# Two operand buffers and seven weight buffers moved to one place modulo 256 bytes in SBUF

## The chip, the cores and the metric

The kernel runs on one NeuronCore of a Trainium2 chip. The metric is device time in microseconds for one launch. Names of engines are those of the profile: PE is the matrix engine, PEld its weight loads (they run beside its matmuls), ACT and DVE the two elementwise engines, POOL the general one, SP the one whose queue issues every DMA of this kernel. SBUF is the on-chip memory of 128 partitions; a buffer begins at the same byte address in every partition. That address modulo 256 is called the buffer's **place** in this document. PSUM is the memory that the matmuls write.

## The reference

Two layers in sequence. The first is attention with a sigmoid in place of the softmax, for 8 batches, 12 heads, 448 positions and head dimension 64. The second is a channel mix with a shift by one position in time.

```python
scores = scale * np.matmul(q, k.transpose(0, 1, 3, 2)) - np.log(S)
attn = 1.0 / (1.0 + np.exp(-scores))
x = np.matmul(attn, v)                      # then heads side by side: (8, 448, 768)
xk = mu_k * x + (1.0 - mu_k) * x_prev       # x_prev is x one position earlier
xr = mu_r * x + (1.0 - mu_r) * x_prev
k = np.maximum(xk @ w_k, 0.0)               # 768 -> 1024
v = k * k @ w_v                             # 1024 -> 768
r = 1.0 / (1.0 + np.exp(-(xr @ w_r)))       # 768 -> 768
return r * v
```

All is float32; the three weight matrices arrive as float64.

## The kernel before, in words

**Attention** (the first 268.6 us of the span). The heads are taken in 48 pairs. Keys and queries are split into a coarse float32r part and a remainder, and a score tile is the sum of three float32r matmuls (coarse by coarse, remainder by coarse, coarse by remainder; `scores`, L338). The two heads of a pair sit in the two halves of the array's rows. The split keys and queries lie in the weight buffers' spare columns (`kk` in slots 0 and 3, `qh` in 1 and 4, `ql` in 2 and 6), because the weight buffers are not full yet. ACT applies the sigmoid (L361), PE weighs the values with it in plain float32 (`weigh`, L368), and ACT and DVE blend each position with the one before (L391, L392). The blended results go to DRAM. Meanwhile the float64 weights come in as raw bits (`wraw`), DVE turns them into float32 (`wbit`), and their combinations are stored to DRAM or put into the slots.

**The three products** (stage 0: `xr @ w_r`, stage 1: `xk @ w_k`, stage 2: `k*k @ w_v`). The 3584 columns are cut into 7 blocks of 512. Each block pair is multiplied with a scheme that needs seven half-size products instead of eight (`ORDER`: products 0, 1, 4, 5, 6, 2, 3); the first, odd block has four plain ones (`SINGLE`: 0, 4, 1, 3). That is 25 products in each stage. Product `p` has its own weight buffer: `slots[POS[p]]`, so in the order of `ORDER` the products use slot 0, 1, 2, 3, 4, 5, 6, and in that of `SINGLE` slot 0, 2, 1, 6. A slot holds a coarse half `hi` and a remainder `lo`, each 1152 or 1536 float32r numbers long in a partition.

The moving operand (512 columns) is split in the same way (`operand`, L453 on ACT and L454 on DVE) into one of two buffers: `rra`, allocated at the kernel's start, or `rrb`, allocated in the attention's space after that is freed. `take` deals them out: in stages 0 and 1 coarse part and remainder of one operand lie in the same buffer, two operands in `rra`, the next two in `rrb`. In stage 2 every third operand has its coarse part in `rra` and its remainder in `rrb`.

`multiply` (L592) issues one matmul with its weight load for each of the three combinations of parts and each tile of 128 rows:

```python
for e, (a, b) in enumerate(((whi[:, c], hi[:, t]), (whi[:, c], lo[:, t]), (wlo[:, c], hi[:, t]))):
    nc.tensor.matmul(bank, a, b, ...)       # a: 128x128 weights, b: 128x512 moving
```

A product of stage 0 has 27 such matmuls, one of stages 1 and 2 has 36; the three stages have 25 x (27 + 36 + 36) = 2475. Products 0, 1, 4 and 2 write the PSUM banks called `xb`, products 5, 6 and 3 those called `yb` (in a block pair: xb, xb, xb, yb, yb, xb, yb). The order on every engine is fixed beforehand by a planner (`Plan`), which lists each operation with a cost and a priority and emits them sorted by the start that it works out. It knows no addresses.

**Where the buffers lie.** The left side of SBUF holds a small constant pool that ends at byte 16672 and then the pool `wp`. Everything in it is a multiple of 256 bytes long, apart from the two tiles called `gap` and the 8 numbers (32 bytes) by which a slot is longer than its content. Every tile of weights and every part of an operand begins a multiple of 256 bytes behind the start of its buffer, so one number gives the place of all that PE reads from it.

Of the kernel before, what the change touches and what calls it, by code (L numbers as in the profile page):

```python
# [8 lines left out]
F32 = mybir.dt.float32  # L9
F32R = mybir.dt.float32r  # L10
# [88 lines left out]
def attention_then_channel_mix(  # L99
# [16 lines left out]
    P = 128  # L116
# [16 lines left out]
    WO = NJH * DF // 2  # L133
# [27 lines left out]
    def ring(pool, name, bufs, shape, dtype):  # L161
        return [pool.tile(shape, dtype, name=f"{name}{i}") for i in range(bufs)]

    wp = ctx.enter_context(tc.tile_pool(name="wp", bufs=1, side="left"))
    att = ExitStack()
    wp.tile([P, 56], F32, name="gap0")
    slots = [wp.tile([P, 2 * WO + 8], F32R, name=f"slot{g}") for g in range(7)]
    wp.tile([P, 8], F32, name="gap1")
    RU = 2 * NJH
    rra = wp.tile([P, 2 * RU, TB], F32R, name="rra")  # L170
    ysa = wp.tile([P, RU, TB], F32, name="ysa")
# [376 lines left out]
    kp = ctx.enter_context(tc.tile_pool(name="kp", bufs=1, side="right", reuse_waits="tile"))  # L548
# [3 lines left out]
    p1s = ring(kp, "p1s", 4, [P, TB], F32)  # L552
    u2 = ring(kp, "u2", 4, [P, TB], F32)
    cc = ring(kp, "cc", 5, [P, TB], F32)
    kp.tile([P, 40], F32, name="gap2")
    pb = ctx.enter_context(tc.tile_pool(name="pb", bufs=1, space=PSUM, reuse_waits="tile"))
    yb = ring(pb, "yb", 4, [P, TB], F32)
    xb = ring(pb, "xb", 4, [P, TB], F32)
# [150 lines left out]
```

## Time and profile before

| | |
|---|---|
| median of 3 runs | 851.38 us (850.54 to 852.36) |
| profiled execution | 849.64 us, of it the span 847.7 us |
| granted PE clock | 1.0 throughout |
| attention, 0 to 268.6 us | PE busy 259.28, DVE 218.51, ACT 202.84, DMA share 0.82 |
| products, 268.6 to 843.3 us | PE busy 574.66 of 574.70, DVE 415.83, ACT 265.77, DMA share 0.56 |
| end, 843.3 to 847.7 us | DVE 1.38, last DMA |

A PE row of the timeline view gives the start of its first matmul, how long it lasted until the modelled end of its last one, the bank written, the moving buffer and the weight buffer (numbers left out) and the count. Because matmuls overlap, the time that a matmul costs is not its own duration but the distance from the start of one row to the start of the next, divided by the count. This is called the **pace** below.

### The profile page before, as it was taken

The numbers are of one execution on the slowest core, as the hardware profiler recorded it, in microseconds if no ns is written. First come the engines' busy times: TensorE is split into PE (matmuls) and PEld (weight loads), VectorE is DVE, ScalarE is ACT, GpSimd is POOL, SyncE is SP. The second block draws the span as 40 slices with busy tenths as digits, with TensorE's granted clock in tenths as the row PEclk, the third lists the DMA queues.
The fourth block names the chain that finished last, engine by engine and source line by source line (L and its number), as shares of the span: only waits on it lengthen the run. The fifth ranks groups of instructions, "written<-read, shape, count | busy, mean of one in ns | idle before, by whom it ended". The sixth has DMA issues, their size and how long they took to land.

```text
span 847.7 us, 12701 instructions
## 1 busy us (share of the span) xinstructions
PE 833.9 (98%) x4299; PEld 591.2 (70%) x4299; DVE 635.7 (75%) x1156; ACT 468.6 (55%) x753; POOL 10.6 (1%) x100
## 2 busy tenths in 40 slices
PE   7999999999989999999999999999999999999997
PEld 4444444444445888888888888888888888888886
DVE  5788989887877889799895375284666748949854
ACT  5788978777775435446447456366574323332320
POOL 0000000000000000000000000000000000000000
PEclk9999999999999999999999999999999999999999
DMA  6778877798987783848784526524755465457304
GB/s 216 248 250 291 292 248 246 252 323 293 311 283 253 278 286 140 256 154 270 268 269 151 173 101 211 161 100 137 272 175 189 133 224 174 136 187 224 124 25 149
DMA packets 97489, 179.64 MB, mean 212 GB/s; under 512 B 12560, under 2 KB 53008, under 8 KB 95632
## 3 DMA queue, kind: packets, MB, share of 16 engines
q1 hardware_dynamic: 97424, 178.83, 63.6%
q8 instruction: 34, 0.56, 0.3%
q14 instruction: 31, 0.25, 0.1%
HBM read 109.06 MB, written 69.73 MB: 211 GB/s over the span
## 4 chain that ended last, share of the span: by engine, by line
PE 94%; DMA 2%; issue 2%; ACT 1%; DVE 1%; DVEq 0%; ACTq 0%
PE xb L592 38%; PE yb L592 30%; PE av L368 12%; PE sc L338 10%; PE av L376 2%; DMA xk_d<-xo 2%; PE sc L349 2%; ACT xo L391 1%; DMA raw<-in_qk 0%; DVE xo L392 0%; ACT pf L361 0%; ACT pt L361 0%; DVE slot L317 0%; DVE cc L647 0%; DVE cc L617 0%
## 5 line engine op out<-in xcount | busy, mean ns | idle before, releaser
L592 PE MATMUL xb<-rra,slot 128*128 128x512 f32 x717 | 177.5, 394 | 0.0
L592 PE MATMUL xb<-rrb,slot 128*128 128x512 f32 x669 | 165.5, 394 | 0.0
L592 PEld LDWEIGHTS xb<-rra,slot 128*128 128x128 f32 x717 | 134.5, 188 | 32.3 <-issue 0.7
L592 PE MATMUL yb<-rra,slot 128*128 128x512 f32 x618 | 154.4, 395 | 0.0
L592 PEld LDWEIGHTS xb<-rrb,slot 128*128 128x128 f32 x669 | 125.6, 188 | 29.3
L361 ACT ACTIVATE pf<-sc 128x896 f32<-128x896 f32 x144 | 123.2, 936 | 22.4 <-PE sc L338 22.4
L592 PEld LDWEIGHTS yb<-rra,slot 128*128 128x128 f32 x618 | 116.3, 188 | 27.3
L368 PE MATMUL av<-pf,vn 128*64 128x448 f32 x576 | 118.6, 547 | 4.5 <-DVE xo L392 4.4
L592 PE MATMUL yb<-rrb,slot 128*128 128x512 f32 x471 | 119.3, 395 | 0.0
L338 PEld LDWEIGHTS sc<-slot,slot 64*128 64x128 f32 x864 | 76.9, 187 | 49.6 <-issue 17.6
L338 PE MATMUL sc<-slot,slot 64*128 64x448 f32 x864 | 106.6, 383 | 4.8 <-DVE slot L317 4.8
L592 PEld LDWEIGHTS yb<-rrb,slot 128*128 128x128 f32 x471 | 88.5, 188 | 21.2
L368 PEld LDWEIGHTS av<-pf,vn 128*64 128x64 f32 x576 | 37.2, 136 | 64.6 <-issue 47.7
L453 ACT CAST rra<-ysa 128x512 fp32r<-128x512 f32 x88 | 52.5, 622 | 51.8 <-PE xb L592 15.0
L454 DVE TENSOR_TENSOR rra<-ysa,rra 128x512 fp32r<-128x512 f32 x76 | 49.9, 686 | 13.0 <-ACT rra L453 12.7
L453 ACT CAST rrb<-ysa 128x512 fp32r<-128x512 f32 x60 | 35.4, 616 | 35.9 <-DVE u L633 10.6
L391 ACT ACTIVATE xo<-av,omr 128x447 f32<-128x447 f32 x48 | 30.7, 639 | 41.5 <-PE av L376 23.4
L318 DVE TENSOR_TENSOR slot<-raw,slot 128x384 fp32r<-128x384 f32 x96 | 52.5, 584 | 0.0
L392 DVE SCALAR_TENSOR_TENSOR xo<-av,mur,xo 128x448 f32<-128x448 f32 x48 | 32.7, 681 | 19.1 <-ACT xo L391 10.7
L633 DVE TENSOR_TENSOR u<-yb,p1s 128x512 f32<-128x512 f32 x30 | 20.7, 691 | 34.9 <-PE yb L592 34.9
L454 DVE TENSOR_TENSOR rrb<-ysa,rrb 128x512 fp32r<-128x512 f32 x60 | 39.0, 684 | 10.4 <-ACT rrb L453 10.1
L578 DVE TENSOR_TENSOR slot<-cc,slot 128x512 fp32r<-128x512 f32 x42 | 28.0, 685 | 19.3 <-ACT slot L577 19.3
(68 smaller groups left out, 789.6 us busy)
## 6 DMA issues: line engine op xcount, KB each, us to landing
raw<-in_qk SPq DMA_DIRECT2D x48, 448.0 KB, 6.4
k_d<-cc SPq DMA_DIRECT2D x56, 256.0 KB, 2.2
vn<-in_v SPq DMA_DIRECT2D x48, 224.0 KB, 2.7
xr_d<-xo SPq DMA_DIRECT2D x48, 224.0 KB, 6.7
xk_d<-xo SPq DMA_DIRECT2D x48, 224.0 KB, 6.5
r_d<-cc SPq DMA_DIRECT2D x42, 256.0 KB, 2.2
out<-cc SPq DMA_DIRECT2D x42, 256.0 KB, 3.1
wraw<-in_moe_w_k SPq DMA_DIRECT2D x12, 512.0 KB, 7.2
```

Of the source, the lines that this page charges most:

```text
L318: op(DVE, dve(w), at, lambda src_=src_, hi=hi, lo=lo: nc.vector.tensor_sub(lo, src_, hi), [R, (key + "h", i)], [(key + "l", i)])
L338: nc.tensor.matmul(sc[u][:, h, :S], kk[i][half[h], int(e == 1), kc], qq[i][half[h], :], start=e == 0, stop=e == 2)
L349: nc.tensor.matmul(sc[u][half[h ^ (m % 2)], m % 2, :S], t[half[h], QKW:], t[half[h], KW:QKW], start=True, stop=True)
L361: op(ACT, act(2 * S), at, lambda: nc.scalar.activation(f, sc[u][:, :, :S], AF.Sigmoid, bias=NEG_LOG_S, scale=SCALE), R, [K])
L368: nc.tensor.matmul(av[n % 2][half[h], :S], vn[n % 5][:, h * NC + c, :], pf[i][:, h, :], start=c == 0, stop=False)
L391: op(ACT, act(S, False, True), at, lambda y=y, om=om: nc.scalar.mul(y[:, 1:], x[:, :S - 1], om[:, j:j + 1]), [("av", n % 2), ("om", key)], ...
L392: op(DVE, dve(S, ptr=True), at - 5, lambda y=y, mu=mu: nc.vector.scalar_tensor_tensor(y, x[:, :S], mu[:, j:j + 1], y, ALU.mult, ALU.add), ...
L453: op(ACT, act(TB, True), at, lambda t=t: nc.scalar.copy(hi[:, t], y[:, t]), [Y[t]], [H[t]])
L454: op(DVE, dve(TB), at, lambda t=t: nc.vector.tensor_sub(lo[:, t], y[:, t], hi[:, t]), [Y[t], H[t]], [L[t]])
L578: op(DVE, dve(TB), at, lambda h_=h_, l_=l_, w=w: nc.vector.tensor_sub(l_, w, h_), [W, K + (h, "hi")], [K + (h, "lo")])
L592: nc.tensor.matmul(bank, a, b, start=first and t == 0 and e == 0, stop=t == n - 1 and e == 2, skip_group_check=True)
L633: op(DVE, dve(TB), at, lambda: add(u2[i], y, p1s[i]), [Y, P1], [U2])
```

## The change

The slots lose their 8 extra numbers, the two gap tiles of the left pool go, and the gap at the end of the right pool `kp` grows from 40 to 48 numbers, which moves that pool's other tiles down by 32 bytes.

```diff
     wp = ctx.enter_context(tc.tile_pool(name="wp", bufs=1, side="left"))
     att = ExitStack()
-    wp.tile([P, 56], F32, name="gap0")
-    slots = [wp.tile([P, 2 * WO + 8], F32R, name=f"slot{g}") for g in range(7)]
-    wp.tile([P, 8], F32, name="gap1")
+    slots = [wp.tile([P, 2 * WO], F32R, name=f"slot{g}") for g in range(7)]
...
     cc = ring(kp, "cc", 5, [P, TB], F32)
-    kp.tile([P, 40], F32, name="gap2")
+    kp.tile([P, 48], F32, name="gap")
     pb = ctx.enter_context(tc.tile_pool(name="pb", bufs=1, space=PSUM, reuse_waits="tile"))
```

The places (byte address modulo 256) in the two built programs:

| buffer | before | after |
|---|---|---|
| slots 0, 1, 2, 3, 4, 5, 6 | 0, 32, 64, 96, 128, 160, 192 | all 32 |
| `rra` (moving operands) | 0 | 32 |
| `rrb` (moving operands) | 64 | 32 |
| `ysa`, `wraw`, `wbit`, `wexpo` | 0 | 32 |
| `ysb`, `p1s`, `u2`, `cc` | 64 | 32 |
| attention's `raw`, `vn`, `pf`, `pt`, `xo` | 224 | 224 |

In all engines' lists the instructions, their order, their shapes and their waits are the same in both programs; they differ in addresses alone.

## The prediction

> **What bounds the kernel now.** I read the busy time by stage first, then the order of PE's matmuls inside the products, then the chain of waits. By stage (columns: span, then busy time and count of PE, PEld, DVE, ACT and POOL, granted clock, DMA share, GB/s):
>
> ```profile
> 0.00:268.60 268.60, 259.28 (x1825) 126.29 (x1825) 218.51 (x459) 202.84 (x289) 10.48 (x99) 1.00 0.82 270
> 268.60:843.30 574.70, 574.66 (x2479) 464.87 (x2475) 415.83 (x697) 265.77 (x464) 0.10 (x1) 1.00 0.56 186
> ```
>
> The second row holds the three products. PE is busy for 574.66 of 574.70 us at the full clock, and all 2475 weight loads fall in it; 574.70 / 2475 = 232.2 ns is what one matmul costs on average. No other engine is near: DVE works 72% of the time. So each nanosecond of pace in these 2475 matmuls is 2.5 us of the kernel, and the question is what the pace hangs on. The timeline of PE shows it, because the name of a row gives the moving buffer, and the sequence of banks gives the product and so the slot:
>
> ```profile
> 500.47 8.58 PE L592 MATMUL xb<-rra,slot 128*128 128x512 f32 x36
> 508.89 8.41 PE L592 MATMUL yb<-rra,slot 128*128 128x512 f32 x36
> 517.14 16.82 PE L592 MATMUL xb<-rrb,slot 128*128 128x512 f32 x72
> ...
> 567.44 8.56 PE L592 MATMUL yb<-rra,slot 128*128 128x512 f32 x36
> 575.84 8.35 PE L592 MATMUL xb<-rra,slot 128*128 128x512 f32 x36
> 584.03 16.76 PE L592 MATMUL xb<-rrb,slot 128*128 128x512 f32 x72
> 600.63 16.96 PE L592 MATMUL yb<-rra,slot 128*128 128x512 f32 x72
> 617.43 8.58 PE L592 MATMUL xb<-rrb,slot 128*128 128x512 f32 x36
> 625.84 8.53 PE L592 MATMUL yb<-rrb,slot 128*128 128x512 f32 x36
> 634.21 8.37 PE L592 MATMUL xb<-rra,slot 128*128 128x512 f32 x36
> 642.42 8.56 PE L592 MATMUL yb<-rra,slot 128*128 128x512 f32 x36
> 650.82 8.55 PE L592 MATMUL xb<-rrb,slot 128*128 128x512 f32 x36
> 659.21 0.39 PE L592 MATMUL yb<-rra,slot 128*128 128x512 f32 x1
> ```
>
> From 575.84 on this is the last block pair of stage 1 (slots 0 to 6) and from 634.21 the first block of stage 2 (slots 0, 2, 1, 6). The rows are of one shape, with nothing idle between them. Start to start, over the count, and beside it the place of the weights less the place of the moving operand (modulo 256):
>
> - 575.84, slot 0 on rra, difference 0: 8.19 / 36 = 227.5 ns. 634.21, the same pair: 8.21 / 36 = 228.1 ns.
> - 642.42, slot 2 on rra, difference 64: 8.40 / 36 = 233.3 ns.
> - 617.43, slot 5 on rrb, difference 96: 8.41 / 36 = 233.6 ns.
> - 625.84, slot 6 on rrb, difference 128: 8.37 / 36 = 232.5 ns.
> - 500.47, slot 5 on rra, difference 160: 8.42 / 36 = 233.9 ns.
> - 508.89, slot 6 on rra, difference 192: 8.25 / 36 = 229.2 ns; 567.44, the same pair: 8.40 / 36 = 233.3 ns.
> - 650.82, slot 1 on rrb, difference 224: 8.39 / 36 = 233.1 ns.
> - 584.03, slot 1 (224) and slot 2 (difference 0, at place 64) on rrb together: 16.60 / 72 = 230.6 ns. With 233.1 for the first, slot 2 is left with 228.1 ns.
>
> The pace is thus a matter of addresses. Where weights and moving operand share a place, be it 0 or 64, it is about 227.8 ns; elsewhere it is 232 to 234, but for one pair that was seen at both 229.2 and 233.3. The before kernel has the shared place in few of its products, since its slots lie at seven different places and its operands at two.
>
> **The change, part by part.**
>
> *Products.* The change gives all weights and all operands place 32, so every one of the 2475 matmuls, the split operands of stage 2 included, has difference 0. If the difference is what counts, each costs 227.8 ns (the mean of 227.5 and 228.1): 2475 x 0.2278 = 563.8 us instead of 574.7, a gain of 10.9. PE never waits in this stretch, so all of it reaches the end as long as the others keep up. The hardest part for DVE is the start:
>
> ```profile
> 260.00:450.00 190.00, 190.00 (x844) 150.41 (x837) 165.96 (x302) 96.14 (x170) 0.44 (x4) 1.00 0.72 243
> ```
>
> DVE has 166 us of work in 190; with PE 2% quicker the same work has 186 us, 89%. That covers it. Were the cover gone and DVE the bound there, the most that could be lost is that stretch's share of the gain, 190 x 1.9% = 3.6 us.
>
> *Attention.* Its score matmuls read slots too. Today their differences (keys in slots 0 and 3, queries in 1, 2, 4 and 6) are 224, 192 and 160, and they become 0. No score matmul at difference 0 is in the trace, so I bound the gain. Two heads' matmuls run side by side, so the 864 of L338 are 432 pairs:
>
> ```profile
> L338 PE MATMUL sc<-slot,slot 64*128 64x448 f32 x864 | 106.6, 383 | 4.8 <-DVE slot L317 4.8
> ...
> 185.62 2.48 PE L368 MATMUL av<-pf,vn 128*64 128x448 f32 x12
> 188.02 2.10 PE L338 MATMUL sc<-slot,slot 64*128 64x448 f32 x18
> 190.05 0.60 PE L368 MATMUL av<-pf,vn 128*64 128x448 f32 x2
> ```
>
> A run of 18 (9 pairs) takes 190.05 - 188.02 = 2.03 us, 225 ns for a pair of only 448 columns, so part of it is not address conflicts but the waits between the planner's operations. If a pair gained the 233.3 - 227.8 = 5.5 ns of the products, 432 of them would gain 2.4 us; if those waits or the attention's stops set the time, nothing. The chain has such stops, in which PE is not the last to arrive:
>
> ```profile
> 99.97 6.78 DMA xk_d<-xo
> 144.54 7.29 DMA xk_d<-xo
> 234.48 3.05 issue x2
> ```
>
> I take 1.0 us, a little under the middle. The other matmuls of the attention (values weighed, score tails) read buffers that stay at place 224.
>
> *Loads, casts, copies.* DMAs and elementwise work now touch place 32 where they touched 0 or 64. The trace has aligned and unaligned neighbours for these:
>
> ```profile
> raw<-in_qk SPq DMA_DIRECT2D x48, 448.0 KB, 6.4
> wraw<-in_moe_w_k SPq DMA_DIRECT2D x12, 512.0 KB, 7.2
> ...
> ysa<-r_d SPq DMA_DIRECT2D x22, 256.0 KB, 3.2
> ysb<-r_d SPq DMA_DIRECT2D x20, 256.0 KB, 3.0
> ...
> L453 ACT CAST rra<-ysa x88: 601/621/711, 79.3 to 795.1; 128x512 fp32r<-128x512 f32 x88
> L453 ACT CAST rrb<-ysa x60: 602/619/647, 270.8 to 784.8; 128x512 fp32r<-128x512 f32 x60
> ```
>
> A load into place 224 moves 448 / 6.4 = 70 KB per us, one into place 0 moves 512 / 7.2 = 71; 256 KB land in place 64 no later than in place 0; a cast into place 0 takes 621 ns, into 64 619. I cost these at nothing; PE's 2475 matmuls hide them, and if the cover were gone, 1.5% (70 against 71) of a 7.2 us load would be 0.1 us.
>
> *Sum.* 10.9 + 1.0 = 11.9 us off the profiled execution's 849.64: 837.7. The median of the runs shown stands 1.7 higher, so 851.38 - 11.9 = **839.5 us**.
>
> **What speaks against it.** After the change both operands lie at place 32, an odd multiple of 32, and no row shows that: the shared places seen are 0 and 64. Odd differences are also slower than their neighbours suggest. Between the even ones (64: 233.3, 128: 232.5, 192: 229.2, 0: 227.8) one would expect 232.9 at 96, 230.9 at 160 and 228.5 at 224; the rows say 233.6, 233.9 and 233.1, or 0.7, 3.0 and 4.6 more, 2.8 on average. In each of these rows exactly one of the two operands is at an odd multiple of 32. It may be the mismatch that costs, which the change removes, or the odd place itself, which it doubles.
>
> **The rivals.**
>
> *The odd place costs on its own, for each operand (slower).* Place: every matmul of L592. Price: two operands at 2.8 ns on top of the shared place, 227.8 + 5.6 = 233.4 ns against 232.2 now, so 2475 x 1.2 ns = 3.0 us more: 854.4 us. It decides from a pace above 232.2. For it: no row with an odd place is under 233. Against it: the rows at differences 64 and 128 have no odd place and are as slow, so oddness isn't needed to explain 233.
>
> *Half of that.* One such price for both operands together: 230.6 ns, 1.6 ns under now, 4.0 us gained, 847.4 us (attention at nothing).
>
> *Places don't matter in themselves (no change): 851.4 us.* The pace would then follow something that goes with the product, such as its place in the block pair or what ACT and DVE do beside it. Against it: 575.84 and 634.21 differ in stage, neighbours and companions and agree to 0.6 ns, and slot 2 is slow on rra (233.3) and quick on rrb (228.1). For it: 508.89 and 567.44, one pair of places at two paces, so the pace has more than one input.
>
> [...]
>
> *A second steady state at the shared place (not quite the gain).* As with 508.89 and 567.44, some products could settle at 233.3. If one in four did, 0.25 x 2475 x 5.5 ns = 3.4 us would be missing: 842.9. All three products at difference 0 in the rows above are quick, so this belongs to the forecast's own spread.
>
> **How the numbers follow.** The forecast, place by difference alone, gets 0.68: its own range is 836.5 (2.4 us in attention and a slightly better pace) to 843. The half price gets 0.12, no change 0.08, the odd place as a loss 0.12. What a measurement of this kernel can tell from no change is about 0.2%, 1.7 us. Faster: 0.68 + 0.12 = 0.80; same 0.08; slower 0.12. The range holds the first two cases and leaves out the others' 0.2: 836 to 849.
>
> **What would show it.** In the changed kernel's timeline every full row of 36 at L592 should stand 8.2 us before the next, whatever its buffers, and the stretch from the first product's matmul to the last should be 564 us with PE still without idle time. Rows of 8.4 throughout mean the odd place costs; a mix of 8.2 and 8.4 means two steady states. Runs of 18 score matmuls should take 1.98 to 2.03 us. If the pace falls but the span doesn't, idle time of PE before L592 would name the engine that is late next, DVE in the first stage before any other. The forecast is wrong if the stretch isn't shorter by at least 7 us.

## The result and the profile after

The changed kernel takes **838.94 us** (median of 4 runs, 838.69 to 839.72) where the kernel before takes 851.87 (4 runs, 850.54 to 853.09): a ratio of 0.985 with a 95% interval of 0.9833 to 0.9867, so 12.9 us or 1.5% faster. The forecast was 839.5.

The profiled execution of the changed kernel took 839.72 us, 837.8 of it the span. By stage (span, then busy time and count of PE, PEld, DVE, ACT and POOL, granted clock, DMA share, GB/s):

```profile
0.00:272.00 272.00, 261.17 (x1824) 127.04 (x1824) 219.83 (x461) 202.76 (x289) 11.04 (x100) 0.99 0.81 267
272.00:833.35 561.35, 561.35 (x2479) 464.60 (x2475) 413.54 (x693) 265.23 (x464) 0.00 (x0) 1.00 0.57 190
```

The products shrank from 574.70 to 561.35 us, 13.35 us less, 226.8 instead of 232.2 ns for each of the 2475 matmuls. PE is busy for all of it, so no engine became late, and the work of DVE and ACT is the same (413.54 and 265.23 us against 415.83 and 265.77). The attention took 3.4 us longer in this execution (272.0 against 268.6); what that is worth is told under the experiments.

The timeline of PE over the last block pair of stage 1 and the first block of stage 2, as it was read before (`multiply` is at L590 now, since two lines fell away; in a stage's first block product 4 writes `yb`, so that its banks come as xb, yb, xb, yb):

```profile
563.90 8.32 PE L590 MATMUL yb<-rra,slot 128*128 128x512 f32 x36
572.07 8.32 PE L590 MATMUL xb<-rra,slot 128*128 128x512 f32 x36
580.23 16.48 PE L590 MATMUL xb<-rrb,slot 128*128 128x512 f32 x72
596.54 16.48 PE L590 MATMUL yb<-rra,slot 128*128 128x512 f32 x72
612.87 8.32 PE L590 MATMUL xb<-rrb,slot 128*128 128x512 f32 x36
621.02 8.32 PE L590 MATMUL yb<-rrb,slot 128*128 128x512 f32 x36
629.18 8.32 PE L590 MATMUL xb<-rra,slot 128*128 128x512 f32 x36
637.35 8.32 PE L590 MATMUL yb<-rra,slot 128*128 128x512 f32 x36
645.50 8.32 PE L590 MATMUL xb<-rrb,slot 128*128 128x512 f32 x36
```

Every row of 36 stands 8.15 to 8.17 us before the next and every row of 72 16.31 to 16.33: 226.4 to 226.9 ns for all slots and both operand buffers. The spread that such rows had before (227.5 to 233.9) is gone.

### The profile page after: what moved, and what is told of

The parts are those of the page before. It is cut to its first block, busy times and chain, and to the rows that moved or that the text cites. A ratio compares the mean times of both kernels' runs of the same rounds, so it can differ in the third digit from the quotient of the medians.

```text
span 837.8 us, 12701 instructions
## 1 busy us (share of the span) xinstructions
PE 822.5 (98%) x4299; PEld 591.6 (71%) x4299; DVE 634.8 (76%) x1156; ACT 468.0 (56%) x753; POOL 11.0 (1%) x100
## 4 chain that ended last, share of the span: by engine, by line
PE 90%; DMA 5%; ACT 2%; issue 1%; DVE 1%; DVEq 0%; SPq 0%; ACTq 0%; POOL 0%; POOLq 0%
PE xb L590 38%; PE yb L590 29%; PE av L366 11%; PE sc L336 9%; DMA xk_d<-xo 4%; PE av L374 2%; PE sc L347 1%; ACT xo L389 1%; ACT pt L359 1%; ACT pf L359 1%; DVE xo L390 1%; DMA raw<-in_qk 0%; DVE slot L315 0%; ACT rra L451 0%; DVE cc L645 0%
## 5 line engine op out<-in xcount | busy, mean ns | idle before, releaser
L590 PE MATMUL xb<-rra,slot 128*128 128x512 f32 x717 | 173.9, 389 | 0.0
L590 PE MATMUL xb<-rrb,slot 128*128 128x512 f32 x669 | 162.2, 389 | 0.0
L590 PEld LDWEIGHTS xb<-rra,slot 128*128 128x128 f32 x717 | 134.5, 188 | 28.6 <-issue 0.7
L590 PE MATMUL yb<-rra,slot 128*128 128x512 f32 x618 | 150.8, 389 | 0.0
L590 PEld LDWEIGHTS xb<-rrb,slot 128*128 128x128 f32 x669 | 125.6, 188 | 26.0
L590 PEld LDWEIGHTS yb<-rra,slot 128*128 128x128 f32 x618 | 116.0, 188 | 24.1
L590 PE MATMUL yb<-rrb,slot 128*128 128x512 f32 x471 | 116.3, 389 | 0.0
L590 PEld LDWEIGHTS yb<-rrb,slot 128*128 128x128 f32 x471 | 88.4, 188 | 18.3
L452 DVE TENSOR_TENSOR rra<-ysa,rra 128x512 fp32r<-128x512 f32 x76 | 49.4, 685 | 11.0 <-ACT rra L451 10.9
```

Source lines behind the costliest of these rows:

```text
L452: op(DVE, dve(TB), at, lambda t=t: nc.vector.tensor_sub(lo[:, t], y[:, t], hi[:, t]), [Y[t], H[t]], [L[t]])
L590: nc.tensor.matmul(bank, a, b, start=first and t == 0 and e == 0, stop=t == n - 1 and e == 2, skip_group_check=True)
```

## The experiments

All paces are read as before, start to start over the count. The diffs are shortened (`...` or a remark marks what is left out). They stand against the changed kernel, and from "Which stream has to walk?" on against the kernel before. Slot and product follow from the sequence of banks.

**One half: the weights at one place.** Slots all at 32, `rra` at 0 and `rrb` at 64 as before.

```diff
     slots = [wp.tile([P, 2 * WO], F32R, name=f"slot{g}") for g in range(7)]
     ...
+    wp.tile([P, 56], F32, name="gap0")          # rra to place 0
     rra = wp.tile([P, 2 * RU, TB], F32R, name="rra")
     ...
-    kp.tile([P, 48], F32, name="gap")
+    kp.tile([P, 40], F32, name="gap")           # rrb to place 64
```

> Slots all at place 32, rra at 0 and rrb at 64 as before: half of the change. Theory (the difference of the places decides): every product has difference 32 or 224, none has 0, so the pace is 233.2 ns throughout, 2475 x (233.2 - 232.2) = 2.5 us slower than before, about 854 us. Rival 1 (it is enough that all weights share a place, because loads follow each other): 226.7 ns as in the changed kernel, 839 us. Rival 2 (both halves add up): half the gain, about 845 us.

Measured: 854.86 us against 850.79, ratio 1.0037 (1.002 to 1.0054). The stretch of the products:

```profile
268.50:846.20 577.70, 577.68 (x2479) 464.38 (x2475) 414.64 (x694) 266.31 (x464) 0.00 (x0) 1.00 0.56 185
```

577.70 / 2475 = 233.4 ns, 3.0 us longer than before. It is not enough that the weights share a place; without difference 0 anywhere, this half alone is a loss.

**The other half: the operands at one place.** `rra` and `rrb` at 32, slots staggered by 32 bytes from 0 to 192.

```diff
-    slots = [wp.tile([P, 2 * WO], F32R, name=f"slot{g}") for g in range(7)]
+    wp.tile([P, 56], F32, name="gap0")
+    slots[0] = wp.tile([P, 2 * WO], F32R, name="slot0")
+    wp.tile([P, 8], F32, name="gap1")           # and so on, 8 before each next slot
+    slots[1] = wp.tile([P, 2 * WO], F32R, name="slot1")
     ...
+    wp.tile([P, 24], F32, name="gap7")          # rra stays at place 32
```

> rra and rrb both at place 32, slots at 0, 32, 64, 96, 128, 160, 192: the other half. Theory (difference): only slot 1 has difference 0 and runs at 226.7 ns; the others have 224, 32, 64, 96, 128 and 160 and run at 232 to 234; weighted by their 4, 4, 4, 3, 3, 3 and 4 products of 25 that is 232.4 ns, as before, 851 to 853 us. Rival (operands that share a place are what helps): all rows at 226.7 ns, 839 us.

Measured: 853.11 us against 850.79, ratio 1.003 (1.0017 to 1.0044). In its timeline the first block of stage 2, with slots 0, 2 and 1 in that order:

```profile
638.40 8.56 PE L605 MATMUL xb<-rra,slot 128*128 128x512 f32 x36
646.80 8.56 PE L605 MATMUL yb<-rra,slot 128*128 128x512 f32 x36
655.20 8.34 PE L605 MATMUL xb<-rrb,slot 128*128 128x512 f32 x36
663.37 0.39 PE L605 MATMUL yb<-rra,slot 128*128 128x512 f32 x1
```

Slot 0 (difference 224) and slot 2 (32) take 8.40 us, 233.3 ns; slot 1 (difference 0) takes 8.17, 226.9 ns. One quick slot of seven is about what the kernel before had, hence no gain. The stretch of the products:

```profile
272.50:847.60 575.10, 575.09 (x2479) 464.85 (x2475) 415.08 (x693) 266.06 (x464) 0.00 (x0) 1.00 0.56 186
```

575.10 us is only 0.4 more than before, so most of the 2.3 us between the medians lies outside the products. In them the two halves do not add up: 3.0 us lost and 0.4 us lost alone, 13.35 us won together. What counts is weights against operand.

**All at place 0 instead of 32.** This tells the difference from the place itself; `rrb` moreover stands 256 bytes off modulo 512.

```diff
+    wp.tile([P, 56], F32, name="gap0")
     slots = [wp.tile([P, 2 * WO], F32R, name=f"slot{g}") for g in range(7)]
     ...
-    kp.tile([P, 48], F32, name="gap")
+    kp.tile([P, 56], F32, name="gap")
```

> Slots, rra and rrb all at place 0; rrb lies 256 modulo 512 from the slots, rra 0 modulo 512. Theory (difference modulo 256 alone): 226.7 ns in every row, whichever buffer, 839 us as with place 32. Rival 1 (place 32 itself is better than 0): rows between 226.7 and 230 ns, up to 847 us. Rival 2 (the period is 512 bytes): rra rows at 226.7, rrb rows at 232 to 234 ns, about 845 us.

Measured: 838.21 us against 850.79, ratio 0.9849 (0.9827 to 0.9871).

```profile
270.80:832.10 561.30, 561.30 (x2479) 464.48 (x2475) 415.63 (x695) 265.45 (x464) 0.10 (x1) 1.00 0.57 190
```

561.30 us against the changed kernel's 561.35, 226.8 ns for each matmul in both: place 0 and place 32 cost the same. Rows on `rra` and rows on `rrb` stand 8.16 us apart for 36 (226.7 ns), so the 256 bytes between `rrb` and the slots cost nothing, where 128 bytes cost 232.5 ns in the kernel before. The odd place 32 has no price of its own, which ends the rival that forecast a loss.

**Small differences.** Operands at 32, slots 0 to 6 at +4, +8, +16, +24, +48, +112 and -16 from them (inside a tile that is 8 numbers longer).

```diff
+    slots[0] = wp.tile([P, 2 * WO + 8], F32R, name="slot0")[:, 1:2 * WO + 1]   # +4 bytes; the others likewise
```

> rra and rrb at place 32; slots 0 to 6 ahead of them by 4, 8, 16, 24, 48, 112 and -16 bytes. Theory (two address streams meet in a memory bank that is some tens of bytes wide): 4 and 8 bytes are as good as 0 (226 to 229 ns), 16 and 24 lie between, 48 and 112 run at 232 to 234, and -16 is within 2 ns of 0. Rival (only exact equality is good): all seven at 232 to 234 ns. In the first case the kernel takes some 844 to 846 us, in the second 853.

Measured: 849.93 us in one execution, beside 850.79. The first block of stage 2 (slots 0, 2, 1) and two rows of stage 1 (slots 5 and 6):

```profile
618.55 8.56 PE L603 MATMUL xb<-rrb,slot 128*128 128x512 f32 x36
626.95 8.33 PE L603 MATMUL yb<-rrb,slot 128*128 128x512 f32 x36
635.12 8.53 PE L603 MATMUL xb<-rra,slot 128*128 128x512 f32 x36
643.49 8.56 PE L603 MATMUL yb<-rra,slot 128*128 128x512 f32 x36
651.89 8.47 PE L603 MATMUL xb<-rrb,slot 128*128 128x512 f32 x36
660.19 0.39 PE L603 MATMUL yb<-rra,slot 128*128 128x512 f32 x1
```

+4: 8.37 / 36 = 232.5 ns; +8: 8.30, 230.6; +16: 8.40, 233.3; +112: 8.40, 233.3. Rows of stage 1 at 543.55 and 551.83 give 8.28, 230.0 ns for +24 and 8.40, 233.3 ns for +48. Only -16 is quick: 8.17, 226.9 ns. The theory of a place some tens of bytes wide fails at +4 and +8, the rival of exact equality fails at -16.

**Behind the operand.** Differences of -4, -8, -12, -24, -40, 0 and +12 on `rra` and 32 less of each on `rrb`, by the same means.

> rra at place 32, rrb at 64; slots 0 to 6 at 28, 24, 20, 8, 248, 32 and 44, so the weights stand at -4, -8, -12, -24, -40, 0 and +12 bytes from an operand in rra and at -36, -40, -44, -56, -72, -32 and -20 from one in rrb. Theory (as the last map showed: weights ahead of the moving operand by a few bytes are dear at once, weights behind by 16 bytes are not): -4, -8 and -12 at 226 to 229 ns, +12 at 230 to 233; somewhere between -16 (227 ns) and -32 (233 ns) the pace jumps, and -36 to -56 lie at 231 to 234. Rival (it is not order but whether both are 16 bytes aligned): -4, -8, -12 at 231 to 233, and all differences that are multiples of 16 apart from 0 and -16 at 233.

Measured: 849.13 us in one execution, beside 850.83. The row of slot 0 in stage 1, then slots 0, 2 and 1 in stage 2:

```profile
575.62 8.55 PE L602 MATMUL xb<-rra,slot 128*128 128x512 f32 x36
584.01 17.04 PE L602 MATMUL xb<-rrb,slot 128*128 128x512 f32 x72
...
634.29 8.32 PE L602 MATMUL xb<-rra,slot 128*128 128x512 f32 x36
642.45 8.33 PE L602 MATMUL yb<-rra,slot 128*128 128x512 f32 x36
650.62 8.33 PE L602 MATMUL xb<-rrb,slot 128*128 128x512 f32 x36
658.79 0.40 PE L602 MATMUL yb<-rra,slot 128*128 128x512 f32 x1
```

Slot 0 on `rra` (-4) takes 8.39 us, 233.1 ns, in the one place and 8.16, 226.7 ns, in the other. In the second place -12 on `rra` and -40 on `rrb` run at 226.9 ns as well. Neither theory foresaw that: one pair of addresses has two steady paces, and the quick one, 226.7, is not reserved for difference 0. What picks the state is not shown; the three quick rows follow one another. In rows of stage 1 of this kernel, -12 on `rra` takes 233.1 ns (533.88), -24 takes 230.8 (542.27), 0 takes 227.5 (500.78), and +12 takes 226.7 in one row (508.97) and 230.0 in another (567.34).

**All weights 16 bytes behind.** Both operand buffers moved on by 16 bytes, slots left at 32, as an attempt to do better than the change.

```diff
-    rra = wp.tile([P, 2 * RU, TB], F32R, name="rra")
+    rra = wp.tile([P, 2 * RU * TB + 8], F32R, name="rra")[:, 4:2 * RU * TB + 4].rearrange("p (u c) -> p u c", c=TB)
     ...                                         # rrb likewise, and the gap at the end of kp back to 40
```

> The changed kernel with both operand buffers 16 bytes further on (place 48; slots stay at 32), so that all weights stand 16 bytes behind. In the first map this difference stood at 227.1 to 227.4 ns among slow neighbours, where difference 0 stood at 227 to 228. If it is a little better than 0: 225 to 226.5 ns throughout, 835 to 838 us. If the two are one and the same: 226.7 ns, 838 to 840 us. If it was a matter of its neighbours: 228 to 232 ns, 843 to 852 us.

Measured: 850.69 us against 851.94, ratio 0.9988 (0.997 to 1.0005), no gain.

```profile
269.50:843.10 573.60, 573.60 (x2479) 465.27 (x2475) 415.52 (x695) 266.35 (x464) 0.00 (x0) 1.00 0.56 186
```

573.60 / 2475 = 231.8 ns. The quick row at -16 in the first map (weights at 16, operand at 32) does not return with weights at 32 and operand at 48, whatever the cause: another state, or the operand's own place below 32 bytes. "The difference decides" is shown for places that are multiples of 32, and not below.

**Which stream has to walk?** A weight load and a matmul each read a stream of columns; it walks when it goes from column to column, and stands when it reads one column again and again. Two kernels with the addresses of the kernel before. In one the weight load reads one column 128 times, in the other the matmul reads one operand column 512 times.

```diff
-    ((whi[:, c], hi[:, t]), (whi[:, c], lo[:, t]), (wlo[:, c], hi[:, t]))
+    ((one(whi), hi[:, t]), (one(whi), lo[:, t]), (one(wlo), hi[:, t]))         # first: one() repeats a column of weights
+    ((whi[:, c], one(hi)), (whi[:, c], one(lo)), (wlo[:, c], one(hi)))         # second: one() repeats a column of the operand
```

> The kernel before with its seven slots at seven places, but each weight load reads one column 128 times instead of 128 columns (so the products compute something else). Theory (the excess over the streaming time of 512 columns is two address streams meeting): a load that doesn't walk meets the moving stream at one place of 256 bytes only, so the differences of places hardly count: all rows within 3 ns of each other, at 227 ns or below, at most 840 us. Rival 1 (a load costs time as such, wherever it reads): the same seven paces as before, 227 to 234 ns, 851 us. Rival 2 (a load that stays in one place is met each time the moving stream comes by): all rows slower than 234 ns.

> The kernel before, but each matmul reads one column of the moving operand 512 times (so the products compute something else); the weight loads walk as before. Theory (two streams meet): the load comes by the one place that the moving operand reads at most twice in its 512 bytes, so all rows lie within 3 ns of each other and at 227 ns or below, at most 840 us. Rival 1 (a load costs time as such): 227 to 234 ns by slot, 851 us. Rival 2 (reading one place over and over blocks the load at each pass): slower than 234 ns.

Measured: 849.72 and 809.28 us, one execution of each, beside 850.83 of before. The products, weights standing and then operand standing:

```profile
269.80:843.30 573.50, 573.50 (x2479) 467.43 (x2475) 415.79 (x696) 265.86 (x464) 0.10 (x1) 1.00 0.56 186
```

```profile
268.50:802.90 534.40, 534.40 (x2479) 468.28 (x2475) 410.56 (x695) 263.85 (x464) 0.10 (x1) 1.00 0.60 200
```

With a standing operand the pace is 534.40 / 2475 = 215.9 ns, the same for every slot (7.77 us for 36 and 15.54 for 72 in every row from 561.87 to 631.80), as expected; the place of the weight loads then makes no difference, though they walk and all 2475 are there. So 11 ns of the changed kernel's 226.8, and 16 of the 232.2 before, belong to the walking operand. With standing weights it is 231.7 ns, again the same for every slot (8.33 to 8.34 us for 36 and 16.68 for 72 from 559.68 to 659.75). The place of the weights thus mattered only where both walk: the seven paces became one in both kernels. But with standing weights it was expected at 227 ns or less and isn't: a load that keeps to one place costs about the average of before.

**Does the walking speed matter?** Weight loads at a step of two columns, addresses of the kernel before.

```diff
-    c = slice(t * w + i * P, t * w + (i + 1) * P)
+    c0 = min(t * w + i * P, n * w - 2 * P)
+    c = slice(c0, c0 + 2 * P, 2)
```

> The kernel before, but each weight load reads 128 columns at a step of two, 1024 bytes instead of 512 (so the products compute something else). Step 0 gave 231.7 ns at all places, and a moving operand that doesn't walk gave 215.8 ns at all places, so the excess is paid when the moving stream passes the load. Theory (a load of step one walks at about half the speed of the moving stream, which passes it about twice in the load's time; at step two both walk at nearly one speed and keep their distance): some differences of places, those far from 0, fall to 216 to 220 ns, and some get worse, above 234; the spread over the slots grows beyond the 6 ns of before. Rival (a load blocks the moving stream for a number of cycles, whatever the two addresses do relative to each other): 226 to 234 ns, no difference below 224 ns, about 851 us.

Measured: 852.45 us in one execution, beside 850.83 of before; the products took 574.9 us, and the slots' paces lie between 229 and 234 ns. No difference of places falls below 224: the rival's numbers hold. That a load walks at about half the speed of the moving operand is an estimate: in the profile of before a load of 128 columns (L592) takes 188 ns and one of 64 (L368, plain float32) takes 136, 52 / 64 = 0.81 ns a column, and the matmul with a standing operand 215.9 / 512 = 0.42. That the streams pass each other and could be kept apart by walking at one speed is not borne out. But the rival's words, that it doesn't matter what the two addresses do, fail too. The first block of stage 2 with slots 0 and 2 on `rra`:

```profile
637.03 8.56 PE L593 MATMUL xb<-rra,slot 128*128 128x512 f32 x36
645.43 8.45 PE L593 MATMUL yb<-rra,slot 128*128 128x512 f32 x36
653.71 8.57 PE L593 MATMUL xb<-rrb,slot 128*128 128x512 f32 x36
```

Slot 0, at difference 0, takes 8.40 us, 233.3 ns, and slot 2, at difference 64, takes 8.28, 230.0 ns. In the kernel before it was 228.1 and 233.3. The shared place is thus the cheap one for weights read column by column, and not for weights read at a step of two.

**Which bits of the operand's address matter?** The operand's first 64 columns (256 bytes) read 8 times, and in another kernel its first 16 (64 bytes) read 32 times; weights and addresses as before.

```diff
+    win = lambda x: x[:, t, :64].unsqueeze(1).broadcast_to((P, TB // 64, 64))   # or 16
-    ((whi[:, c], hi[:, t]), (whi[:, c], lo[:, t]), (wlo[:, c], hi[:, t]))
+    ((whi[:, c], win(hi)), (whi[:, c], win(lo)), (wlo[:, c], win(hi)))
     ...
+    nc.tensor.matmul(bank[:, :].rearrange("p (r c) -> p r c", c=64), a, b, ...)   # the bank written in the same order; or 16
```

> As the run before with 64 columns (256 bytes) read 8 times: the moving operand goes through the same 256 bytes again and again instead of 2048 bytes in a row. Theory (the place modulo 256 is all that counts): the paces of the kernel before, slot by slot, 227 to 234 ns, 232 on average, 850 to 852 us. Rival (the range of addresses counts, or reading afresh): a pace clearly lower, towards 215.8.

> The kernel before, but each matmul's moving operand is its first 16 columns (64 bytes) read 32 times, so it walks, yet only within a quarter of the 256 bytes (the products compute something else); loads as before. Theory (the two streams lose time where they are in the same part of the 256 bytes): the load is in that quarter for about a quarter of its time, so about a quarter of the excess of 11 to 18 ns over 215.8 is left: 218 to 221 ns, 815 to 822 us. Rival (the load takes a fixed number of turns from a moving operand that fetches at all): 227 to 234 ns, about 851 us.

Measured: 852.26 us with 256 bytes, 879.20 with 64, beside 851.72 of before. The 256-byte kernel over the last block pair of stage 1:

```profile
578.46 8.35 PE L593 MATMUL xb<-rra,slot 128*128 128x512 f32 x36
586.65 16.76 PE L593 MATMUL xb<-rrb,slot 128*128 128x512 f32 x72
603.25 16.96 PE L593 MATMUL yb<-rra,slot 128*128 128x512 f32 x72
620.05 8.58 PE L593 MATMUL xb<-rrb,slot 128*128 128x512 f32 x36
628.47 8.53 PE L593 MATMUL yb<-rrb,slot 128*128 128x512 f32 x36
```

Durations of 8.35, 16.76, 16.96, 8.58 and 8.53 us are those of the kernel before, figure for figure, though other addresses were read. The products take 574.70 us, as before. So the bits of the operand's address above bit 7 changed nothing here, and reading data afresh didn't either. With 64 bytes the products take 600.2 us, 242.5 ns, the opposite of the expected 218 to 221: an operand confined to a quarter of the 256 bytes loses more, not less. Going back to the start 8 times cost nothing in the 256-byte kernel (574.70 us both); whether going back 32 times does was not tested apart.

**Only where both read the same part?** Weights standing at place 32 x slot, the operand confined to its first 32 columns (128 bytes), addresses of the kernel before.

```diff
+    win = lambda x: x[:, t, :32].unsqueeze(1).broadcast_to((P, TB // 32, 32))
+    ((one(whi), win(hi)), (one(whi), win(lo)), (one(wlo), win(hi)))           # one() and the bank as above
```

> The kernel before, where a weight load reads one column 128 times (place 0, 32, ... 192 by slot) and the moving operand is its first 32 columns read 16 times, so that it stays within 128 of the 256 bytes: places 0 to 127 in rra, 64 to 191 in rrb (the products compute something else). Theory (time is lost only where both streams read the same part of the 256 bytes): no loss, 215.8 ns, for slots 4, 5, 6 on rra and 0, 1, 6 on rrb, whose load lies outside; 231 ns and more, since the moving operand comes by twice as often as with step 0 alone, for slots 0 to 3 on rra and 2 to 5 on rrb. Rival (the loss goes with how the moving operand is fetched, not with where the load is): the same pace for all slots.

Measured: 863.09 us in one execution beside 854.73 of before. The same block pair:

```profile
585.00 8.64 PE L594 MATMUL xb<-rra,slot 128*128 128x512 f32 x36
593.48 17.12 PE L594 MATMUL xb<-rrb,slot 128*128 128x512 f32 x72
610.44 17.12 PE L594 MATMUL yb<-rra,slot 128*128 128x512 f32 x72
627.40 8.64 PE L594 MATMUL xb<-rrb,slot 128*128 128x512 f32 x36
635.88 8.64 PE L594 MATMUL yb<-rrb,slot 128*128 128x512 f32 x36
```

8.48 us for 36 and 16.96 for 72, 235.6 ns in each of these rows, whether the standing load lies inside the operand's 128 bytes (slots 0 and 3 on `rra`, 2 and 5 on `rrb`) or outside (4 on `rra`, 1 and 6 on `rrb`). The rival holds, and the theory that time is lost only where both streams read the same part of the 256 bytes falls.

**The attention's length.** The attention of the six kernels with standing, stepped or windowed reads has the very addresses of the kernel before. Its length, from the stage rows, is 268.6 us before, 269.8 and 268.5 with standing weights and operand, 271.2 with weights at a step of two, and with windows of 64, of 256 and of 128 bytes:

```profile
0.00:272.60 272.60, 261.25 (x1824) 126.88 (x1824) 219.86 (x461) 203.09 (x289) 10.67 (x100) 0.99 0.80 266
```

```profile
0.00:271.20 271.20, 260.72 (x1825) 126.55 (x1825) 219.83 (x461) 202.86 (x289) 11.90 (x100) 0.99 0.81 268
```

```profile
0.00:273.20 273.20, 261.95 (x1824) 127.21 (x1824) 219.84 (x461) 203.09 (x289) 11.65 (x100) 0.99 0.80 266
```

So with one set of addresses it varies from 268.5 to 273.2 us, and the 272.0 of the changed kernel's profile needs no cause in the change. The half with the weights at one place, whose score matmuls read the very places of the changed kernel's, took 268.5. What the length goes with is the granted clock: in the stage rows of all these profiles an attention at 1.00 takes 268.5 to 270.8 us, one at 0.99 takes 271.2 to 273.2. In the changed kernel's profile the clock falls near the end of the attention:

```profile
250.00:256.00 6.00, 4.07 (x32) 2.42 (x30) 5.73 (x12) 5.13 (x8) 0.10 (x1) 0.96 0.65 206
256.00:260.00 4.00, 4.00 (x24) 2.22 (x20) 3.93 (x8) 1.01 (x2) 0.34 (x3) 0.64 0.65 244
```

The kernel before has 1.00 in both stretches. Its PE was busy for 259.28 us of the attention, that of the changed kernel for 261.17, so 1.9 of the 3.4 us are matmuls that took longer; 6 us at 0.96 and 4 us at 0.64 lose 6 x 0.04 + 4 x 0.36 = 1.7 us by estimate, so the clock accounts for most of that. The other 1.5 us are idle time of PE. Why the clock falls in some executions and not in others is not shown.

Taken from the medians instead, the rest of the kernel beside the products is 851.87 - 574.70 = 277.2 us before and 838.94 - 561.35 = 277.6 after: no change that these runs can tell.

## Why the prediction was right

**What bounds the kernel.** As read: PE is busy for 561.35 of 561.35 us, and every nanosecond of pace passed through.

**The products' term.** Mechanism right, size a little low: 13.35 us gained instead of 10.9. The shared place was priced by the quick rows of before, 227.8 ns, and came to 226.8. Those rows stood between products at other differences, and the changed kernel's rows stand among their like. The trace of before shows such a row settle, when the one at 575.84 is cut after its sixth matmul:

```profile
577.22 6.97 PE L592 MATMUL xb<-rra,slot 128*128 128x512 f32 x30
```

Its first six matmuls take 577.22 - 575.84 = 1.38 us, 230 ns each, and the other thirty, up to 584.03, take 6.81 us, 227.0 ns each. So the quick pace was there before; a product reached it only after some matmuls, and the mean of the row priced it 1 ns too high.

**The attention's term.** Wrong: 1.0 us was taken, at most 0.5 came. The changed kernel's runs of 18 score matmuls, as undisturbed as those quoted before:

```profile
179.21 2.09 PE L336 MATMUL sc<-slot,slot 64*128 64x448 f32 x18
181.23 2.48 PE L366 MATMUL av<-pf,vn 128*64 128x448 f32 x12
```

181.23 - 179.21 = 2.02 us against 2.03. That is 0.01 us a run, at most 0.5 us over 48 runs and below what the whole time can tell, so the lower bound (nothing) was about right: with keys and queries at one place a run still takes 2.02 us. What sets that was not tested. The misses, 2.4 us too little in the products and 0.5 to 1.0 too much in the attention, partly cancel, and the median of before moved from 851.38 to 851.87. That 839.5 stands so near to 838.94 is luck; the mechanism and most of the size are not.

**Loads, casts and copies at nothing.** Nothing contradicts it: in the products DVE works 413.54 us and ACT 265.23 (415.83 and 265.77 before), PE is busy in all 561.35 us, `raw` lands in 6.2 us (6.4 before) and `wraw` of `w_k` in 6.6 (7.2), and a cast into `rra` takes 622 ns (621).

**The covered start.** It held; PE didn't idle in the first stage or later.

**The rivals.** The odd place's own price, whole or half, is refuted twice: by the changed kernel itself and by the kernel at place 0, 561.35 and 561.30 us. The excess at odd differences that gave it its price (233.1 to 233.9 ns) is gone where weights and operand share the odd place 32 (226.8), so it went with the mismatch. "No change" is refuted by the change itself, which changes nothing but places and takes 13.35 us from the products, and by the half that moves only the weights, which adds 3.0. By the addresses read alone one shape ran at 226.8 ns (the changed kernel), 233.4 (its weights alone at one place) and 215.9 (a standing operand), so here the weight load's reads and the matmul's did bear on each other.

A second steady state exists, as 508.89 and 567.44 had hinted, and the maps show it at 226.7 and 233.1 ns for one pair of addresses. It is no accident of one execution. The kernel with the 256-byte window has the slow row of 567.44 again, in the same product, 8.40 us before the next at 578.46:

```profile
570.06 8.56 PE L593 MATMUL yb<-rra,slot 128*128 128x512 f32 x36
```

In the changed kernel only the first product is slow as a whole, 6.30 us for 27 matmuls or 233 ns, and it settles on the way:

```profile
272.01 6.46 PE L590 MATMUL xb<-rra,slot 128*128 128x512 f32 x27
274.68 3.79 PE L590 MATMUL xb<-rra,slot 128*128 128x512 f32 x16
278.31 6.28 PE L590 MATMUL yb<-rra,slot 128*128 128x512 f32 x27
```

The second line is the first cut after its eleventh matmul: the last sixteen take 278.31 - 274.68 = 3.63 us, 226.9 ns each. No later product of this kernel left that pace (226.4 to 226.9 ns, row by row), and at place 0 the mean of all products is 226.8 ns.

**What stays open.** Why a walking operand costs 11 ns a matmul and more, why a shared place is the cheap case, and what picks the state elsewhere. Four ideas were put to the chip (a place tens of bytes wide, order of the two streams, passing at different speeds, reading the same part at the same time) and each failed on at least one run. What stands is empirical: the time was lost with a walking operand (226.7 ns and more, 215.9 with a standing one); only the bits of its address below 256 bytes counted (574.70 us of products with the 256-byte window and without); and how much was lost depended on the weights' place only when the weights walked too (227.5 to 233.9 ns by slot, 231.7 for every slot when they stood), and then also on the step at which they did (difference 0 at 228.1 ns with a step of one, 233.3 with a step of two).

## What to carry to other kernels

Where PE is busy throughout, the pace from start to start, product by product, is worth setting beside the buffers' addresses modulo 256: rows of one shape at 227 and 233 ns in one profile named most of the gain before anything was changed. For this kernel's float32r matmuls with their own weight loads, weights and operands all at place 32, or all at place 0, gave 226.8 ns instead of 232.2 on average; aligning only the weights lost 3.0 us in the products, and aligning only the operands won nothing (575.10 us against 574.70). A rule read from rows holds as far as the rows reach: at 4 to 16 bytes (230.6 to 233.3 ns with weights 4 to 16 ahead of the operand, 231.8 with all of them 16 behind), for weights read at a step of two (233.3 ns at difference 0), and in the attention's matmuls (2.02 us a run against 2.03), the same reasoning failed.

## What the runs showed of the hardware that was not expected

- A matmul of 512 float32r columns whose operand stands still ran at 215.9 ns with its weight load walking; with a walking operand no product of the other kernels was clearly under 226.7 ns.
- Standing weights were not cheaper than walking ones: 231.7 ns at all seven places, against 226.8 with weights that walk from the operand's own place.
- One pair of addresses ran at 233.1 ns in one product and at 226.7 in another of the same execution (weights 4 bytes behind the operand). In stage 1, the product with slot 6 on `rra` that ran at 233.3 ns in the kernel before (row 567.44) ran at 233.3 again in another execution, with the 256-byte window (row 570.06).
- A product at a shared place reached 227 ns only after some matmuls in the two rows that follow slower work: six in the row of before, eleven at the start of the changed kernel's products.
- With weights read at a step of two, the shared place ran at 233.3 ns and difference 64 at 230.0.
- An operand confined to 64 of the 256 bytes was the slowest of all, 242.5 ns on average.
